# Other y buffers, an earlier copy of a half tile and later gathers in a retention and mixture-of-experts kernel

## The chip, the core and the metric

The kernel runs on one core of one Trainium2 chip. A core has TensorE (PE; its weight loads are listed apart as PEld), VectorE (DVE), ScalarE (ACT), GpSimd (POOL) and SyncE (SP, which here only issues transfers). Each engine works through its own list of instructions in order, and waits on semaphores where it needs another's result. The metric is the device time of one launch in microseconds (us), the median of several runs; lower is better.

## The reference, cut to what matters

```
x = retention(q, k, v)                      # 8 batches x 576 tokens -> x is (4608, 512)
expert_idx = argmax(normalised x @ normalised expert_emb.T / tau)   # one of 8 experts
gate_w = softmax probability of that expert
for e in range(8):
    mask = expert_idx == e
    h = relu(x[mask] @ w1[e])               # (n, 512) @ (512, 1024)
    out[mask] = gate_w[mask, None] * (h @ w2[e])   # (n, 1024) @ (1024, 512)
```

Every token goes to exactly one expert. All is float32.

## The kernel before, in words

The first part, up to about 170 us of the trace, computes the retention and the routing: each token gets a slot in its expert's table of 640 slots, five tiles of 128 (`CT` = 5). The tables `gid` and `sid` hold the token of each slot, for gathering rows of x and for scattering rows of the output. The change touches nothing there.

Then the experts 0 to 7 come one after the other, each with a first product (x by w1) and a second product (h by w2). Float32 numbers are split into a high and a low part, so that each product runs as three passes: high by high, high by low and low by high. ScalarE makes the high part by a copy, VectorE the low part by a subtraction. This is done for x (`xhigh`, `xlow`), for the weights (`w1hi`, `w1lo`, `w2hi`, `w2lo`) and for the hidden rows `hs` (`settle`).

**The first product** of experts 1 to 7 is done as 28 small products (`product(e, n, i)`: form n of 1 to 7, block i of 0 to 3) in the order of the list `ORDER`; below they are called product 1 to product 28 by their place in it. Each is six matmuls over 288, 304 or 320 columns, by the number of rows in the expert's fifth tile. For every block i, products of form 1, 6, 7 and 4 add up in one PSUM bank. After form 1, 6 and 7 ScalarE copies that bank to an SBUF buffer (`ya`, `yb` and `yc` in `follow`), VectorE adds another bank to it, and one or two products later `settle` turns it into the high and low parts of `hs`. The next product of the block writes the bank again, so it waits for the copy: product 20, which is (7, 2), waits for ScalarE's copy after product 17, which is (6, 2). The buffers are the same five `ys[0]` to `ys[4]` that hold the output tiles 0 to 4 of the second product, from which the scatters read.

**The second product** (`mm2(e, i, tasks)`) runs tile by tile. A full tile is 24 matmuls over 512 columns. ScalarE then scales the bank by the gate into `ys[i]`, and GpSimd scatters these rows to the output (`put_rows`). The fifth tile of experts 1 to 6 has a register `rest[e]`, its number of rows: over 64 it runs in full; with 1 to 64 rows it runs 16 matmuls on `ht`, a copy in which the high and the low parts of the half-filled tile stand side by side (`both_parts`, four VectorE copies at L1331); with none it is skipped. In the trace experts 1, 5 and 6 run in full, 2 and 3 run the 16 matmuls, 4 skips its tile. After the half-filled case a second scatter (`add_low`) adds the other half's rows.

**The order** is written out by hand. `mm2_plan(e)` says which tasks stand behind which third of each second-product tile: key 3 i + k stands in tile i, after 8 matmuls (k = 0), after 16 (k = 1) or after the tile's scatter (k = 2). The tasks prepare the next expert n = e + 1 (`xjoin`, `xsums`, `xhigh`, `xlow`, `w1sum`, `w1hi`, `w1lo`) and fetch the rows for the one after that (`gather`, GpSimd) and the gates (`gather_gates`). `mm1_plan` does the same between the small products, with `xturn` at product 10 for block 3 of gathered rows, at 16, 24 and 28 for the blocks 1, 2 and 4: ScalarE rearranges the gathered rows (L408) and SyncE starts their transposing transfer (L409).

Of the kernel before, what the change touches and what calls it, by code (L numbers as in the profile page):

```python
# [29 lines left out]
CT = 5  # L30
# [65 lines left out]
def retention_moe(ctx: ExitStack, tc: tile.TileContext, qk, kn, v0s, vs, w1, w2, head, cst, out):  # L96
# [28 lines left out]
    def done(ps):  # L125

        if Banks.loose is not None:
            Banks.loose.append(ps)
# [14 lines left out]
    ys = [keep.tile([P, DM], F32, name=f"y{k}") for k in range(5)]  # L143
# [216 lines left out]
    def fitted(e, i):  # L360
        return i == CT - 1 and 0 < e < NE - 1
# [189 lines left out]
    with ExitStack() as att:  # L551
# [3 lines left out]
        a1 = att.enter_context(tc.tile_pool(name="a1", bufs=1))  # L555
# [551 lines left out]
    with ExitStack() as moe:  # L1107
# [104 lines left out]
        def settle(src, f, k, queue=lows, bank=False):  # L1212

            hi, lo = (hs[:, s, f].rearrange("p (i h c) -> p h i c", h=2, c=HB)[:, k] for s in range(2))

            def low_part():
                nc.vector.scalar_tensor_tensor(  # L1217
                    out=lo, in0=part(src), scalar=0.0, in1=hi.bitcast(F32), op0=ALU.max, op1=ALU.subtract
                )
                if bank:  # L1220
                    done(src)

            def high_part():
                nc.scalar.activation(hi, part(src), AF.Relu)  # L1224
                queue.append(low_part)

            return high_part

        def settle_last():

            h, l = list(highs), list(lows)
            highs.clear()
            lows.clear()
            for task in h + l:
                task()
# [36 lines left out]
        def follow(n, i):  # L1272

            def add(out, x):
                nc.vector.tensor_tensor(out=out[:, :HC], in0=x[:, :HC], in1=out[:, :HC], op=ALU.add)  # L1275

            ya, yb, yc = ys[min(i, 1)], ys[(2, 3, 2, 4)[i]], ys[0]
            if n in (1, 6, 7):
                nc.scalar.copy({1: ya, 6: yb, 7: yc}[n][:, :HC], Y[i][:, :HC])  # L1279
            if n == 2:  # L1280
                add(ya, W[i])
                done(W.pop(i))
            elif n == 7:
                add(yc, Z[i])
            elif n == 3:
                add(yb, Z[i])
                done(Z.pop(i))
            settle_last()
            if n == 2:
                highs.append(settle(ya, i, 0))  # L1290
            elif n == 7:
                highs.append(settle(yc, NPR + i, 1, held if i == NPR - 1 else lows))
            elif n == 4:
                settle(Y.pop(i), NPR + i, 0, bank=True)()
            elif n == 3:
                highs.append(settle(yb, i, 1))
# [93 lines left out]
        def mm2_plan(e):  # L1390
            n = e + 1
            own, sums = slice(0, 1), slice(1, 3)
            if n == NE:
                return {0: [(count_beyond,)], 3: [(half_rows,)]}
            plan = {
                0: [(xjoin, n, 0)],
                1: [(xsums, n, 0), (xhigh, n, 0, own), (xlow, n, 0, own), (xjoin, n, 1), (w1sum, n, 0), (xhigh, n, 0, sums)],
                2: [(w1hi, n, 0, True), (xsums, n, 1), (xlow, n, 0, sums), (xhigh, n, 1, own), (w1lo, n, 0, True)],
                3: [(xjoin, n, 2), (xlow, n, 1, own), (xhigh, n, 1, sums)],
                4: [(w1hi, n, 0, False), (xsums, n, 2), (xlow, n, 1, sums), (w1lo, n, 0, False)],  # L1400
                5: [(xhigh, n, 2, own), (xjoin, n, 3), (xlow, n, 2, own), (xhigh, n, 2, sums)],
                6: [(w1sum, n, 1), (xhigh, n, 3, own), (xsums, n, 3), (w1hi, n, 1, True), (xjoin, n, 4)],
                7: [(w1lo, n, 1, True), (xlow, n, 3, own), (xhigh, n, 3, sums), (xsums, n, 4), (xlow, n, 2, sums)],
                8: [(xhigh, n, 4, own), (xlow, n, 4, own), (xlow, n, 3, sums), (xhigh, n, 4, sums), (w1hi, n, 1, False)],
                9: [(xlow, n, 4, sums), (w1lo, n, 1, False)],
                10: [(w1sum, n, 2)],
                11: [(w1hi, n, 2, True), (w1lo, n, 2, True)],
                12: [],
            }
            if n + 1 < NE:  # L1410
                for i in range(CT):
                    plan[(2, 4, 8, 9, 11)[i]].append((gather, n + 1, i))
            if fitted(e, CT - 1):
                plan[9].insert(1, (both_parts,))
            for k, a0, a1 in ((2, 0, 2), (5, 2, 4), (9, 4, CT)):
                plan[k].insert(0, (gather_gates, n, a0, a1))
            if n + 1 < NE:
                plan[12].append((xturn, n + 1, 0))
            if e == 0:
                plan[0] = [(xturn, 1, 4)] + plan[0]  # L1420
            return plan

        def mm1_plan(e):
            n = e + 1
            plan = {
                2: [(w2hi, e, 0)],
                3: [(w2lo, e, 0)],
                5: [(w1hi, e, 2, False)],
                6: [(w1lo, e, 2, False), (w1sum, e, 3)],
                12: [(w1hi, e, 3, True)],  # L1430
                13: [(w1lo, e, 3, True)],
                14: [(w1hi, e, 3, False)],
                15: [(w1lo, e, 3, False)],
                18: [(w2hi, e, 1)],
                19: [(w2lo, e, 1)],
                21: [(w2hi, e, 2)],
                22: [(w2lo, e, 2)],
            }
            if n < NE:
                plan[10] = [(xturn, n, 3)]  # L1440
                plan[16] = [(xturn, n, 1)]
                plan[24] = [(xturn, n, 2)]
                plan[28] = [(xturn, n, 4)]
            return plan
# [13 lines left out]
        for f, ps in zip(PAIRS, first):  # L1458
            mm1_out(f, 0, ps)

        plan = {
            4: [(w2hi, 0, 0)],
            5: [(w2lo, 0, 0)],
            6: [(xprep, 0, 3), (xprep, 0, 4), (gates_exp,)],
            7: [(w2hi, 0, 1)],
            8: [(gates_sum,), (w2lo, 0, 1)],
            9: [(w2hi, 0, 2), (gather, 1, 3), (gather, 1, 4)],
            10: [(gates_out,), (w2lo, 0, 2), (xturn, 1, 0)],
            11: [(w2hi, 0, 3)],
# [9 lines left out]
        for e in range(NE):  # L1479
            if e:  # L1480
                plan = mm1_plan(e)
                for k, (n, i) in enumerate(ORDER, 1):
                    product(e, n, i)
                    follow(n, i)
                    if k == 10 and fitted(e - 1, CT - 1):
                        add_low(e - 1)
                    if k < len(ORDER):
                        run_tasks(plan, k)
                highs.pop()()
                w2hi(e, 3)  # L1490
                lows.pop()()
                w2lo(e, 3)
                held.pop()()
                run_tasks(plan, len(ORDER))
            plan = mm2_plan(e)
            for i in range(CT):
                if (e, i) == (0, 2):
                    load_left()
                if e * CT + i == NA - 2:
                    ntile = nc.values_load(ovt[0:1, 0:1], min_val=0, max_val=NO)  # L1500
                mm2(e, i, lambda k: run_tasks(plan, 3 * i + k))
# [196 lines left out]
```

## Time and profile before

| | us |
|---|---|
| median of 3 runs (552.21 to 553.76) | 552.37 |
| the profiled execution's own time | 551.17 |
| its span, first to last instruction | 549.1 |

| engine | busy, us | share of the span |
|---|---|---|
| PE | 541.6 | 99% |
| PEld (weight loads) | 489.4 | 89% |
| DVE | 419.9 | 76% |
| ACT | 377.4 | 69% |
| POOL | 250.9 | 46% |

A row of a timeline gives start, duration, engine, line, operation, the tile written and those read, the shapes and a count of merged instructions; in brackets the engine's idle time before it and what ended that. Line numbers are those of the kernel before. The granted TensorE clock is full in all of the span. The profiled execution's time stands 2.1 us above its span and 1.2 us below the median of the runs.

### The profile page before, as it was taken

How to read it: one execution, taken by the hardware profiler on the slowest of the kernel's cores; microseconds unless marked ns; L12 is line 12 of the kernel's file. 1: busy time of each engine (PE TensorE's matmuls, PEld its weight loads, DVE VectorE, ACT ScalarE, POOL GpSimd, SP SyncE). 2: the span in 40 equal slices, each digit the busy share in tenths (PEclk: the TensorE clock that was granted, in tenths of full speed). 3: DMA queues.
4: the chain of work that ended last, by engine and by line, in shares of the span. 5: the costliest groups of instructions: out<-in, count | busy, mean ns of one | idle time of the engine just before them, and what ended most of it. 6: DMA issues, size and time to landing. Idle time of an engine off the chain costs nothing. (4 is left out here: it accounts for less than half of the span.)

```text
span 549.1 us, 13547 instructions
## 1 busy us (share of the span) xinstructions
PE 541.6 (99%) x5051; PEld 489.4 (89%) x5051; DVE 419.9 (76%) x975; ACT 377.4 (69%) x700; POOL 250.9 (46%) x239
## 2 busy tenths in 40 slices
PE   9999999999999999999999999999999999999996
PEld 8898988989898899889988987998898899889985
DVE  4856788798876957995897889689888958976810
ACT  1257454547758859977896898789789868957511
POOL 6773435553463751285057318704731851334022
PEclk9999999999999999999999999999999999999999
DMA  9999999978458474847556655675665565632111
GB/s 325 407 383 369 371 330 356 378 275 274 160 186 206 161 203 117 166 146 185 159 167 168 164 163 175 183 159 161 184 164 157 173 174 154 137 135 64 66 39 50
DMA packets 81974, 109.79 MB, mean 200 GB/s; under 512 B 43094, under 2 KB 44538, under 8 KB 81888
## 3 DMA queue, kind: packets, MB, share of 16 engines
q1 hardware_dynamic: 71920, 86.24, 51.4%
q0 software_dynamic: 8560, 20.16, 11.9%
q10 hardware_dynamic: 1408, 2.17, 1.1%
q8 instruction: 63, 1.03, 0.7%
q14 instruction: 23, 0.19, 0.1%
HBM read 80.27 MB, written 21.51 MB: 185 GB/s over the span
## 5 line engine op out<-in xcount | busy, mean ns | idle before, releaser
L1349 PE MATMUL m<-w2s,hs 128*128 128x512 f32 x552 | 127.2, 389 | 0.0
L1349 PEld LDWEIGHTS m<-w2s,hs 128*128 128x128 f32 x552 | 103.4, 188 | 21.3
L1309 POOL DMA_INDIRECT out<-y,sid x41 | 45.7, 1115 | 166.1 <-ACT y L1375 134.1
L1349 PE MATMUL a<-w2s,hs 128*128 128x512 f32 (+1 forms) x360 | 78.8, 375 | 0.0
L1349 PEld LDWEIGHTS a<-w2s,hs 128*128 128x128 f32 x360 | 64.2, 188 | 11.9
L366 POOL DMA_INDIRECT raw<-xd,gid x40 | 42.9, 1073 | 19.4 <-issue 9.3
L1224 ACT ACTIVATE hs<-y 128x320 fp32r<-128x320 f32 x84 | 39.2, 473 | 13.1 <-DVE y L1275 12.5
L415 ACT COPY raw<-raw 128x1024 uint16<-128x1024 uint16 x35 | 47.7, 1363 | 0.0
L734 POOL TENSOR_TENSOR kt<-kt,cs 128x512 f32<-128x512 f32 x28 | 28.4, 1044 | 42.1 <-DMA kt<-kn 42.1
L380 POOL DMA_INDIRECT gt<-gd,gid x34 | 39.0, 1146 | 17.2 <-issue 9.7
L1152 DVE TENSOR_TENSOR w2s<-raw,w2s 128x1024 fp32r<-128x1024 f32 x32 | 39.1, 1222 | 8.3 <-ACT w2s L1149 8.2
L1275 DVE TENSOR_TENSOR y<-a,y 128x320 f32<-128x320 f32 x53 | 25.5, 486 | 26.0 <-issue 11.4
L1217 DVE SCALAR_TENSOR_TENSOR hs<-y,hs 128x320 fp32r<-128x320 f32 x84 | 42.3, 510 | 3.3 <-ACT hs L1224 1.3
L1255 PE MATMUL m<-xsb,w0s 128*128 128x288 f32 (+2 forms) x270 | 43.8, 300 | 0.1
L1255 PE MATMUL a<-xsb,w0s 128*128 128x288 f32 (+2 forms) x270 | 43.6, 301 | 0.2 <-ACT y L1279 0.2
L1255 PEld LDWEIGHTS a<-xsb,w0s 128*128 128x128 f32 x270 | 39.2, 188 | 0.4 <-ACT y L1279 0.4
L1255 PEld LDWEIGHTS m<-xsb,w0s 128*128 128x128 f32 x270 | 39.2, 188 | 0.3 <-DVE hs L1217 0.3
L1375 ACT ACTIVATE y<-m,gt 128x512 f32<-128x512 f32 x26 | 17.8, 686 | 31.0 <-PE m L1349 31.0
L408 ACT COPY raw<-raw 128x1024 uint16<-128x1024 uint16 x35 | 36.6, 1045 | 0.0
L1149 ACT CAST w2s<-raw 128x1024 fp32r<-128x1024 f32 x32 | 33.4, 1043 | 2.4 <-DMA raw<-w 2.4
L753 POOL TENSOR_TENSOR qkt<-qkt,gsb 128x384 f32<-128x384 f32 x32 | 31.3, 1008 | 6.5 <-issue 4.2
L454 DVE TENSOR_TENSOR xsb<-raw,xsb 128x128 fp32r<-128x128 f32 x70 | 30.4, 484 | 0.0
(274 smaller groups left out, 1216.9 us busy)
## 6 DMA issues: line engine op xcount, KB each, us to landing
raw<-w SPq DMA_DIRECT2D x64, 512.0 KB
qkt<-qk SPq DMA_DIRECT2D x28, 576.0 KB
xd<-y SPq DMA_DIRECT2D x36, 256.0 KB
vt<-vs SPq DMA_DIRECT2D x7, 1152.0 KB
kt<-kn SPq DMA_DIRECT2D x7, 1024.0 KB
qkt<-qk ACTq DMA_DIRECT2D x4, 288.0 KB
qkt<-qk SPq DMA_DIRECT2D x4, 288.0 KB
out<-y,sid POOLq DMA_INDIRECT x41
```

Source lines behind the costliest of these rows:

```text
L366: nc.gpsimd.indirect_dma_start(out=t[:, XO : XO + DM], out_offset=None, in_=xd[:rows, :], in_offset=bass.IndirectOffsetOnAxis(ap=gid[:, a ...
L380: nc.gpsimd.indirect_dma_start(out=g[:, i : i + 1], out_offset=None, in_=gd[:, :], in_offset=bass.IndirectOffsetOnAxis(ap=ids, axis=0),)
L408: nc.scalar.copy(far.rearrange("p (h n) -> p h n", h=2), near.rearrange("p (n h) -> p h n", h=2))
L415: nc.scalar.copy(far.bitcast(U16).rearrange("p (n h) -> p h n", h=2), near.rearrange("p (h n) -> p h n", h=2))
L753: nc.gpsimd.tensor_tensor(out=q, in0=q, in1=gsb[:, p, :], op=ALU.mult)
L1149: nc.scalar.copy(hi, u)
L1152: nc.vector.tensor_tensor(out=lo, in0=u, in1=hi.bitcast(F32), op=ALU.subtract)
L1217: nc.vector.scalar_tensor_tensor(out=lo, in0=part(src), scalar=0.0, in1=hi.bitcast(F32), op0=ALU.max, op1=ALU.subtract)
L1224: nc.scalar.activation(hi, part(src), AF.Relu)
L1255: nc.tensor.matmul(ps[:, :n_cols], w[:, ws, ka, d * P : (d + 1) * P], xop(kx, xsp)[:, d, :n_cols], start=(n in (1, 2, 5) and d == 0 and k ...
L1309: put = nc.gpsimd.indirect_dma_start(out=out.rearrange("t (k n) -> (t k) n", k=k), out_offset=bass.IndirectOffsetOnAxis(ap=rows, axis=0), ...
L1349: nc.tensor.matmul(ps[:, :step], rows[f // NPR][:, f % NPR] if rows is ht else rows[:, f], w[:, ws, f, n : n + step], start=(m == 0), stop ...
```

## The change

Three edits in the second stage of the kernel. First, `both_parts` moves from the middle of the fourth tile to the head of the second product, behind the first eight matmuls. Second, the gathers of the blocks 2 and 3 and the last gate gather move behind the fourth tile's scatter, block 3 ahead of block 2. Third, the buffers of the first product are dealt out anew: block 1 uses `ys[1]` for both `ya` and `yb`, and blocks 2 and 3 use `ys[3]` for `ya`, which before was `yb` of block 1.

```diff
@@ -1274,7 +1274,7 @@
             def add(out, x):
                 nc.vector.tensor_tensor(out=out[:, :HC], in0=x[:, :HC], in1=out[:, :HC], op=ALU.add)
 
-            ya, yb, yc = ys[min(i, 1)], ys[(2, 3, 2, 4)[i]], ys[0]
+            ya, yb, yc = ys[(0, 1, 3, 3)[i]], ys[(2, 1, 2, 4)[i]], ys[0]
             if n in (1, 6, 7):
                 nc.scalar.copy({1: ya, 6: yb, 7: yc}[n][:, :HC], Y[i][:, :HC])
             if n == 2:
@@ -1408,11 +1408,11 @@
                 12: [],
             }
             if n + 1 < NE:
-                for i in range(CT):
-                    plan[(2, 4, 8, 9, 11)[i]].append((gather, n + 1, i))
+                for i in (0, 1, 3, 2, 4):
+                    plan[(2, 4, 11, 11, 11)[i]].append((gather, n + 1, i))
             if fitted(e, CT - 1):
-                plan[9].insert(1, (both_parts,))
-            for k, a0, a1 in ((2, 0, 2), (5, 2, 4), (9, 4, CT)):
+                plan[0].append((both_parts,))
+            for k, a0, a1 in ((2, 0, 2), (5, 2, 4), (11, 4, CT)):
                 plan[k].insert(0, (gather_gates, n, a0, a1))
             if n + 1 < NE:
                 plan[12].append((xturn, n + 1, 0))
```

VectorE at the head of a second product, where the first product's last low parts end and the next expert's sums (L426, L432) begin; `y_84` to `y_88` are `ys[0]` to `ys[4]`, `raw_77` to `raw_83` the seven buffers `raws[0]` to `raws[6]`:

```order
 L1152 TENSOR_TENSOR w2s<-raw_77,w2s 128x1024
 L1217 SCALAR_TENSOR_TENSOR hs<-y_84,hs 128x5x64
+L1331 COPY w0s<-hs 128x8x32 x4
 L426 TENSOR_TENSOR raw_78<-raw_78 128x256
 L432 TENSOR_TENSOR raw_78<-raw_78 128x128
```

The four copies into `ht` (part of `w0s`) now stand ahead of all of the next expert's sums instead of behind them.

GpSimd behind the third tile's scatter (out<-y_86), in the same second product:

```order
 L380 DMA gt<-gd,gid 128x1 x2
 L1309 DMA out<-y_86,sid 4608x512
-L366 DMA raw_80<-xd,gid 128x512
-L380 DMA gt<-gd,gidx 128x1
-L366 DMA raw_81<-xd,gid 128x512
-L1309 DMA out<-y_87,sid 4608x512
+L1309 DMA out<-y_87,sid 4608x512
+L380 DMA gt<-gd,gidx 128x1
+L366 DMA raw_81<-xd,gid 128x512
+L366 DMA raw_80<-xd,gid 128x512
 L366 DMA raw_82<-xd,gid 128x512
```

The fourth scatter (out<-y_87) moves ahead of two gathers and a gate gather, and the gathers into `raw_80` (block 2) and `raw_81` (block 3) change places.

ScalarE around products 8 to 10 of a first product; `a_` and `m_` are PSUM banks:

```order
 L1224 ACTIVATE hs<-y_85 128x5x64
 L1279 COPY y_84<-a_67 128x320
-L1279 COPY y_87<-m_70 128x320
-L1264 UNCONDITIONAL_BRANCH x5
-L1224 ACTIVATE hs<-y_84 128x5x64
-L1279 COPY y_85<-m_69 128x320
+L1264 UNCONDITIONAL_BRANCH x2
+L1279 COPY y_85<-m_70 128x320
+L1224 ACTIVATE hs<-y_84 128x5x64
+L1264 UNCONDITIONAL_BRANCH x3
+L1279 COPY y_87<-m_69 128x320
 L408 COPY raw_81<-raw_81 128x1024
```

The copies after products 9 and 10 keep their places and exchange buffers: the one after product 9 now writes `y_85`, whose low part VectorE has still to make, and the one after product 10 writes `y_87`.

## Rows read from the trace of the kernel before

**Rows 1.** Waits of PE from 165 to 545 us: total, times, longest.
```profile
PE m L1349 <- DVE w0s L1331: 0.4, 2, 0.2
PE a L1255 <- PEq L1369: 0.3, 1, 0.3
PE a L1255 <- ACT y L1279: 0.2, 1, 0.2
```
**Rows 2.** Timeline of PE, second products of experts 2 and 3.
```profile
281.70 11.04 PE L1349 MATMUL m<-w2s,hs 128*128 128x512 f32 x48
292.95 4.00 PE L1349 MATMUL m<-w2s,w0s 128*128 128x512 f32 x16 [0.21 <-DVE w0s L1331]
...
325.00 5.60 PE L1349 MATMUL a<-w2s,hs 128*128 128x512 f32 x24
330.44 11.04 PE L1349 MATMUL m<-w2s,hs 128*128 128x512 f32 x48
341.64 3.98 PE L1349 MATMUL m<-w2s,w0s 128*128 128x512 f32 x16 [0.16 <-DVE w0s L1331]
```
**Rows 3.** Timeline of DVE in the second product of expert 2.
```profile
275.75 0.43 DVE L426 TENSOR_TENSOR raw<-raw 128x256 f32<-128x256 f32 x1 [0.58 <-ACT raw L415]
...
292.21 1.05 DVE L1331 CAST w0s<-hs 128x256 fp32r<-128x256 f32 x4
```
**Rows 4.** Timeline of DVE in the first product of expert 2.
```profile
255.96 0.52 DVE L1217 SCALAR_TENSOR_TENSOR hs<-y,hs 128x320 fp32r<-128x320 f32 x1
```
**Rows 5.** Timeline of ACT in the first product of expert 2.
```profile
255.84 0.43 ACT L1279 COPY y<-a 128x320 f32<-128x320 f32 x1 [0.32 <-PE a L1255]
256.17 0.47 ACT L1224 ACTIVATE hs<-y 128x320 fp32r<-128x320 f32 x1
256.69 0.43 ACT L1279 COPY y<-m 128x320 f32<-128x320 f32 x1
...
260.03 0.47 ACT L1224 ACTIVATE hs<-y 128x320 fp32r<-128x320 f32 x1 [0.19 <-DVE y L1275]
...
262.98 0.43 ACT L1279 COPY y<-m 128x320 f32<-128x320 f32 x1
```
**Rows 6.** Timeline of ACT in the first products of experts 3, 4 and 6.
```profile
307.74 0.43 ACT L1279 COPY y<-a 128x320 f32<-128x320 f32 x1 [0.28 <-PE a L1255]
...
359.94 0.43 ACT L1279 COPY y<-m 128x320 f32<-128x320 f32 x1
...
457.46 0.42 ACT L1279 COPY y<-m 128x320 f32<-128x320 f32 x1
```
**Rows 7.** Timeline of PE at product 20 of experts 2, 4 and 6.
```profile
263.63 0.96 PE L1255 MATMUL m<-xsb,wsa 128*128 128x288 f32 x6
...
360.62 0.96 PE L1255 MATMUL m<-xsb,w0s 128*128 128x288 f32 x6
...
458.36 1.85 PE L1255 MATMUL m<-xsb,w0s 128*128 128x304 f32 x12
```
**Rows 8.** Timeline of POOL from the second product of expert 2 on.
```profile
293.44 1.77 POOL L380 DMA_INDIRECT gt<-gd,gidx  x1 [0.30 <-issue]
295.51 0.96 POOL L366 DMA_INDIRECT raw<-xd,gid  x1 [0.30 <-DVE wsum L1175]
296.77 1.01 POOL L1309 DMA_INDIRECT out<-y,sid  x1 [0.30 <-issue]
```
**Rows 9.** Timeline of ACT: fourth tile of expert 2 gated; L408 in expert 3.
```profile
292.78 0.69 ACT L1375 ACTIVATE y<-m,gt 128x512 f32<-128x512 f32 x1 [1.63 <-PE m L1349]
...
305.35 1.05 ACT L408 COPY raw<-raw 128x1024 uint16<-128x1024 uint16 x1
```
**Rows 10.** Stretch 297 to 303 us: time, busy PE, PEld, DVE, ACT, POOL, clock, DMA share, GB/s.
```profile
297.00:303.00 6.00, 6.00 (x47) 6.00 (x46) 3.16 (x5) 4.76 (x8) 3.68 (x3) 1.00 1.05 230
```
**Rows 11.** Branches of line L1264 on PE's sequencer: shortest, median, longest in ns.
```profile
L1264 PEldq COMPARE_BRANCH  x224: 70/208/1583, 193.8 to 514.3; - x112
```

## The prediction

> **What bounds the kernel now.** The table of busy times first: PE is busy in 541.6 of 549.1 us, so the time can only fall where PE waits, and can only rise where PE gets a new wait. VectorE (76%), ScalarE (69%) and GpSimd (46%) have room on average, but share their queues between work that PE waits for and work that it doesn't. The second view is the list of PE's waits in the expert stage [rows 1]: only three kinds are listed, 0.9 us together by the page's count. The two at the half-filled fifth tile end with VectorE's copies at L1331; one follows the branch at L1369 where expert 4's tile is skipped; one follows a ScalarE copy in expert 5. The third view, PE's timeline, prices them better. A tile of 24 matmuls takes 5.44 us from start to start (330.44 less 325.00), so two tiles begun at 281.70 should be over at 292.58; the 16 matmuls of expert 2 begin at 292.95, 0.37 us late. For expert 3, 330.44 and two tiles give 341.32, and it begins at 341.64, 0.32 us late [rows 2].
>
> **Edit 1, the copies at the head.** Four copies take 1.05 us; those that PE waits for at 292.95 began only at 292.21 [rows 2, 3]. At the head they stand four tiles, 21.8 us, ahead of the fifth, so this wait goes: at least the idle time that the page shows (0.21 and 0.16), at most the lateness, 0.37 + 0.32 = 0.69 us. I take 0.69, since the copies are then done long before. Nothing is behind them to take their place: the fourth tile's matmuls end at 292.58, and PE then needs only weights and `ht`. The four other fitted experts gain nothing, as PE doesn't read `ht` there. The price is VectorE's: everything from the first sums to the old place is up to 1.05 us later, less the 0.58 us for which VectorE stood idle there [rows 3], so about 0.5 us. PE needs none of that work before the next first product, and from the old place on VectorE is as early as before or earlier. I cost it at nothing; were the cover gone it would be 0.5 us for each of six experts, 3 us.
>
> **Edit 2, the gathers.** Before, the third gather, the gate gather and the gather of block 3 stood ahead of the fourth scatter, which was issued at 296.77 [rows 8], though its tile was ready at 292.78 + 0.69 = 293.47 [rows 9]. Now it goes out at about 293.8, some 3 us earlier, and its buffer `ys[3]` comes free earlier. The gather of block 3, at 295.51 before, now starts behind scatter (1.0) and gate gather (1.8) with 0.3 of issue each: 293.8 + 1.3 + 2.1 = 297.2 at most, 1.7 us later. Block 2's comes 1.3 us after that. Block 3 is wanted by ScalarE's L408 at 305.35 [rows 9], 8 us after the new issue; block 2 not before product 24. PE waits for none of the scatters. Cost nothing; the bounds are a gain of 0.3 us (the wait on ScalarE in expert 5, [rows 1]) and the late gathers below.
>
> **Edit 3, the buffers.** This is the part that adds a wait. ScalarE's copy after product 9 now writes `ys[1]`, from which VectorE still makes a low part; in expert 2 that ends at 255.96 + 0.52 = 256.48 [rows 4], and the copy ran at 255.84 [rows 5]. It has to wait some 0.65 us. Queued behind it on ScalarE are a high part and the copy after product 10. From a copy to the next instruction is 0.33 us (256.17 less 255.84), and the same again behind the high part, so the copy after product 10 starts at 256.5 + 0.66 = 257.2, against 256.69: 0.5 us later. What went before was the same wait one copy later, on the same low part, which is why the shift is 0.5 and not 0.65.
>
> How far does the 0.5 go? In expert 2 ScalarE has a single idle gap from there to the copy after product 17, 0.19 us at 260.03, and that one waits for a VectorE addition that itself follows a ScalarE copy, so it doesn't absorb it. The copy after product 17 started at 262.98 and ended at 263.41 [rows 5]; product 20, which writes the same bank, started at 263.63 [rows 7]. The slack is 0.22, the shift 0.5: a new PE wait of about 0.3. In expert 4 the copy ends at 360.37 [rows 6] and product 20 starts at 360.62 [rows 7], slack 0.25, so again about 0.25 to 0.3. In expert 3 ScalarE is idle for 0.28 us on PE before 307.74 [rows 6], which takes half of the shift, and the rest meets a like slack: nothing. In expert 6 the columns are more and PE slower: copy over at 457.88, product at 458.36 [rows 6, 7], slack 0.48, nothing; experts 1 and 5 stand like it, and expert 7 has no L408 in between. Together about 0.6 us; the bounds are 0, if the shift is absorbed, and the whole delay for all seven experts, 7 x 0.65 = 4.6 us. I take 0.6 because the rows of experts 2 and 4 show both ends of the wait.
>
> The sum: -0.69 + 0.6 = about -0.1 us. Made against the profiled execution it is 551.17 - 0.1 = 551.1; that execution stands 1.2 us below the median of the runs, so the median would go from 552.37 to 552.3.
>
> **The rivals.**
>
> *Only the gain is seen.* ScalarE's queue has small gaps that I counted as dependent; should they absorb the 0.5 us, 0.69 remain, and with expert 5's 0.3 it is 1.0 us: 551.4 to 551.7. For it speaks that PE showed only one wait on ScalarE's copies in seven first products [rows 1], against it that the slack at product 20 is 0.22 us [rows 5, 7].
>
> *ScalarE's new wait decides.* The place is the copy after product 9 in experts 1 to 7, the price up to 0.65 us each, 4.6 in all, less 0.69: 556.3. It decides from where the shift exceeds the slack at product 20 by more than PE can hide; half of the price would be 554.0. Against it speak the slack of 0.48 in expert 6 [rows 6, 7] and that nothing carries over from one expert to the next, because ScalarE catches up in PE's long tiles (1.63 us idle at 292.78, [rows 9]).
>
> *The gathers come late.* Between 297 and 303 us the transfers are at a share of 1.05, all 16 engines full [rows 10], and block 3's gather is now issued at the edge of this stretch instead of before it. If it landed only 2 us after 305.35, ScalarE would stand for that at product 10 and PE for perhaps 1 us of it, six times: 6 us, 558. Against it: even to the end of the stretch there are 2.3 us to spare. The Trainium skill, "DMA: Bandwidth & Descriptors", section "Issuing engines are not separate DMA queues", says that transfers of all issuing engines run on the same 16 engines and interleave; by that rule the later gather shares them with SyncE's transposing transfers, which makes this rival possible, and the share of 1.05 agrees with it.
>
> *The copies aren't what holds the fifth tile.* If PE meets something else at the branch, as in expert 4 where 0.3 us is put down to the sequencer [rows 1], the gain is 0 and only the 0.6 stays: 553.0.
>
> *Code loading.* ScalarE's, VectorE's and GpSimd's lists are cut anew between the branches, with a few rows more; PE's list is the same. One branch on PE's sequencer took 1.58 us where the median is 0.21 [rows 11]. Such a wait at a bad place on ScalarE in each of six experts, with half of it hidden, would be 6 x 0.8 = 4.8 us: 557. The Trainium skill, "Runtime: NRT & Kernel Launch", section "Instruction fetch mechanics", says that a taken branch whose target isn't among the loaded pages must wait for a load; by that rule each moved branch is a risk, and the 1.58 us looks like one such case, though no row shows one on ScalarE.
>
> **How the numbers follow.** A run of this kernel can tell about 0.3%, 1.66 us, from no change. My forecast of about no change has a chance of 0.50; only the gain 0.26; ScalarE's wait 0.09; late gathers 0.06; the copies not to blame 0.06; code loading 0.03. All the PE time that this change can give back is 0.69 + 0.3 = 1.0 us, less than 1.66, so faster gets only 0.06, for what the runs scatter. Slower takes most of ScalarE's wait, the late gathers and code loading and a little of the rest: 0.15. The rest, 0.79, is within 0.3%. Predicted 552.3 us; the forecast's own range is 551.6 to 553.0; the range for 8 in 10 takes in the gain alone, the scatter of the runs and the milder half of ScalarE's wait, 551.0 to 554.1.
>
> **What would show it.** Right: no wait of PE on L1331 any more, and the 16 matmuls of experts 2 and 3 start 10.88 us after the third tile; the copy after product 9 starts as the low part ends, product 20 of experts 2 and 4 waits for ScalarE by 0.2 to 0.4 us; the fourth scatter is issued 3 us earlier and ScalarE's L408 at product 10 doesn't wait. Wrong: an idle ScalarE before that L408, PE waits on ScalarE's copies in most experts, or a span that changes by more than 1.7 us.

## The result, and the profile after

The changed kernel takes 555.47 us (median of 22 runs, 553.43 to 560.93), the kernel before in the same runs 551.96 us: a ratio of 1.0073, with a 95% interval of 1.0058 to 1.0087. It is slower by 0.7%, outside the predicted range. Its profiled execution took 557.73 us, span 555.9 against 549.1.

That execution is one of the slower ones, with a span 6.8 us longer where the medians lie 3.5 us apart, so what follows accounts for one execution and not for the median. Where the 6.8 us went is read by PE's starts. "PE's loss" is below the sum, over the matmuls of the seven first products, of what two starts lie further apart than usual in that stage.

| stretch of the profiled execution | before | after | difference |
|---|---|---|---|
| start to the first product of expert 1 | 197.83 | 199.80 | +1.97 |
| PE's loss in the seven first products | 0.90 | 6.72 | +5.82 |
| late starts of the two half-filled fifth tiles | 0.69 | 0.00 | -0.69 |
| all the rest | | | -0.3 |

The first line is code that the change doesn't touch. It varied between 196.5 and 200.1 us over the fourteen kernels of this study, and what part of it is chance stays open. The other lines are the change. PE's list of waits in the expert stage, which was three short lines [rows 1], is now (total, times, longest):

```profile
PE m L1255 <- ACT y L1279: 1.9, 5, 0.5
PE a L1255 <- ACT y L1279: 0.8, 3, 0.4
PE a L1255 <- PEq L1369: 0.3, 1, 0.3
PE a L1255 <- issue: 0.2, 1, 0.2
```

The two waits on L1331 are gone; there are eight waits on ScalarE's copies (L1279) instead of one. PE's timeline at the fifth tiles of experts 2 and 3, which answers to [rows 2]:

```profile
285.50 11.05 PE L1349 MATMUL m<-w2s,hs 128*128 128x512 f32 x48
296.38 3.89 PE L1349 MATMUL m<-w2s,w0s 128*128 128x512 f32 x16
...
335.62 11.05 PE L1349 MATMUL m<-w2s,hs 128*128 128x512 f32 x48
346.50 3.90 PE L1349 MATMUL m<-w2s,w0s 128*128 128x512 f32 x16
```

Both begin 10.88 us after the third tile, to the hundredth: edit 1 gave all of its 0.69 us. The loss is in the first products. ScalarE in expert 2, where the copy after product 9 is the first row (it answers to the first three of [rows 5]) and the copy after product 17 the last:

```profile
259.84 0.43 ACT L1279 COPY y<-a 128x320 f32<-128x320 f32 x1 [1.83 <-DVE hs L1217]
260.16 0.47 ACT L1224 ACTIVATE hs<-y 128x320 fp32r<-128x320 f32 x1
260.53 0.42 ACT L1279 COPY y<-m 128x320 f32<-128x320 f32 x1
...
266.79 0.42 ACT L1279 COPY y<-m 128x320 f32<-128x320 f32 x1
```

The same place on VectorE (to [rows 4]), on POOL, and PE at product 20 (to the first of [rows 7]):

```profile
258.87 0.85 DVE L1217 SCALAR_TENSOR_TENSOR hs<-y,hs 128x320 fp32r<-128x320 f32 x1
```
```profile
258.64 1.69 POOL L1175 TENSOR_TENSOR wsum<-raw 128x256 f32<-128x256 f32 x2 [3.19 <-DVE wsa L1152]
```
```profile
267.26 1.05 PE L1255 MATMUL m<-xsb,wsa 128*128 128x288 f32 x6 [0.46 <-ACT y L1279]
```

Read them from the start of product 1, 248.44 before and 250.92 after. The low part of `ya` of block 1 ended at 8.04 before, and ends at 8.80 now. The copy after product 9 stands 0.12 behind it, at 8.92. The copy after product 10 goes from 8.25 to 9.61, the one after product 17 from 14.54 to 15.87, and product 20 from 15.19 to 16.34. So the new wait is where the prediction put it, and the chain behind it is the predicted one. But what is waited for is itself later, by 0.76 us. The copy after product 9 starts 0.1 us behind that low part in all seven experts, at 8.35 to 9.86.

Edit 2 on POOL, and the tile that the fourth scatter (first row) waited for, on ScalarE; they answer to [rows 8, 9]:

```profile
297.55 1.14 POOL L1309 DMA_INDIRECT out<-y,sid  x1 [1.84 <-ACT y L1375]
...
300.99 0.98 POOL L366 DMA_INDIRECT raw<-xd,gid  x1 [0.31 <-issue]
```
```profile
296.58 0.69 ACT L1375 ACTIVATE y<-m,gt 128x512 f32<-128x512 f32 x1 [1.50 <-PE m L1349]
...
405.19 0.42 ACT L1279 COPY y<-m 128x320 f32<-128x320 f32 x1
407.09 1.05 ACT L408 COPY raw<-raw 128x1024 uint16<-128x1024 uint16 x1 [1.49 <-DMA raw<-xd,gid]
```

The scatter goes out 0.28 us after its tile is ready, and the gather of block 3 follows 3.44 us later, both as worked out. In expert 5 the last row shows that this gather came too late: L408 at product 10 stood 1.49 us for it. In the other experts L408 follows the copy before it without a gap.

One more loss stands in expert 4: product 15 starts 0.40 us late, 0.51 with the next matmul, behind a branch of line L1267 on PE's sequencer (shortest, median and longest in ns):

```profile
361.78 1.07 PE L1255 MATMUL a<-xsb,w0s 128*128 128x288 f32 x6 [0.23 <-issue]
```
```profile
L1267 PEldq COMPARE_BRANCH  x252: 65/176/1825, 196.1 to 521.8; - x126
```

### The profile page after: what moved, and what is told of

Same layout as the page of the kernel before. It is cut to its first block, busy times and chain, and to the rows that moved or that the text cites. A ratio compares the mean times of both kernels' runs of the same rounds, so it can differ in the third digit from the quotient of the medians.

```text
span 555.9 us, 13555 instructions
## 1 busy us (share of the span) xinstructions
PE 544.2 (98%) x5051; PEld 489.5 (88%) x5051; DVE 419.8 (76%) x975; ACT 375.3 (68%) x700; POOL 252.2 (45%) x239
## 4 chain that ended last, share of the span: by engine, by line
PE 68%; DMA 9%; ACT 8%; DVE 6%; issue 5%; POOL 2%; POOLq 0%; SPq 0%; ACTq 0%
PE m L1349 18%; PE a L1349 11%; PE a L1255 7%; DMA out<-y,sidx 6%; PE m L1255 5%; PE a L763 4%; PE m L763 2%; PE a L846 2%; ACT hs L1224 2%; PE m L465 2%; PE a L465 2%; PE m L846 2%; ACT w0s L1149 2%; DVE y L1275 2%; PE a L929 1%
## 5 line engine op out<-in xcount | busy, mean ns | idle before, releaser
L366 POOL DMA_INDIRECT raw<-xd,gid x40 | 44.3, 1108 | 19.4 <-issue 9.4
L380 POOL DMA_INDIRECT gt<-gd,gid x34 | 40.2, 1183 | 17.1 <-issue 9.8
L408 ACT COPY raw<-raw 128x1024 uint16<-128x1024 uint16 x35 | 36.6, 1047 | 1.5 <-DMA raw<-xd,gid 1.5
```

What stands on the lines that cost most here:

```text
L366: nc.gpsimd.indirect_dma_start(out=t[:, XO : XO + DM], out_offset=None, in_=xd[:rows, :], in_offset=bass.IndirectOffsetOnAxis(ap=gid[:, a ...
L380: nc.gpsimd.indirect_dma_start(out=g[:, i : i + 1], out_offset=None, in_=gd[:, :], in_offset=bass.IndirectOffsetOnAxis(ap=ids, axis=0),)
L408: nc.scalar.copy(far.rearrange("p (h n) -> p h n", h=2), near.rearrange("p (n h) -> p h n", h=2))
```

## The experiments

For the first four runs, theory A: the y buffers alone make the loss. B: the later gathers do. C: it takes both. Then H: PE's completion signals come late where gathers run at the start of a stage. W: the new wait costs the same whatever the transfers do. V: the moved copies make VectorE late. The last column of the table is the stretch from the first product of expert 1 to that of expert 7, which leaves out the first part and the end.

| kernel | ratio to before, 95% interval | PE's loss, us | stretch, us |
|---|---|---|---|
| before | 1 | 0.90 | 295.30 |
| changed | 1.0073, 1.0058 to 1.0087 | 6.72 | 300.14 |
| y_only | 1.0039, 1.0018 to 1.0060 | 3.80 | 298.16 |
| no_y | 1.0002, 0.9977 to 1.0028 | 3.75 | 297.18 |
| copies_only | 1.0080, 1.0053 to 1.0106 | 5.88 | 299.29 |
| gathers_only | 1.0029, 1.0005 to 1.0052 | 0.87 | 294.96 |
| after_no_late | 1.0070, 1.0044 to 1.0097 | 1.93 | 295.37 |
| copies_no_late | 1.0054, 1.0037 to 1.0072 | 0.10 | 293.58 |
| spread | 1.0036, 1.0013 to 1.0058 | 3.86 | 299.28 |
| after_spread | 1.0031, 1.0016 to 1.0045 | 3.04 | 296.71 |
| before_extra | 1.0054, 1.0035 to 1.0072 | 2.63 | 296.52 |
| late4 | 1.0043, 1.0028 to 1.0059 | 3.73 | 297.27 |
| spread_no_y | 1.0044, 1.0028 to 1.0061 | 2.63 | 298.14 |
| spread8 | 1.0179, 1.0134 to 1.0225 | 11.63 | 305.10 |

The losses and stretches are of one profiled execution each. That of gathers_only was the fastest of its 12 runs (550.38, median 554.57), that of before_extra as fast as any of its 8 (551.85, median 553.79), so these two traces show less than the medians. Those of the changed kernel (557.73, median 555.47), spread (556.22, median 553.08) and spread_no_y (554.86, median 553.10) were slow ones and show more.

**One edit alone, and all but one.** y_only:

```diff
-            ya, yb, yc = ys[min(i, 1)], ys[(2, 3, 2, 4)[i]], ys[0]
+            ya, yb, yc = ys[(0, 1, 3, 3)[i]], ys[(2, 1, 2, 4)[i]], ys[0]
```

> The kernel before with the y buffers alone. Theory A (the buffers do it): ScalarE's copy after product 9 waits for VectorE's low part in all seven experts, product 20 waits for ScalarE in most of them, PE loses 3 to 6 us in the first products, no wait on L1331 goes; 555 to 558 us, ratio 1.006 to 1.010. Theory B (the later gathers do it, by making the work around product 5 late): the low part of ya(1) ends 8.0 to 8.3 us after product 1 as before, the loss stays at the 0.6 us of the forecast; ratio 1.000 to 1.002. Theory C (it takes both: the buffers add the wait, the gathers make what is waited for late): about half, ratio 1.002 to 1.005.

no_y is the changed kernel with this line as it was.

> The changed kernel with the y buffers of before: copies at the head and late gathers remain. Theory A: the 0.7 us of the two fifth tiles is gained and nothing is lost, 551 to 552 us, ratio 0.998 to 1.000, PE's loss in the first products near the 0.9 us of before. Theory B: the loss stays, ratio 1.005 to 1.008. Theory C: the work around product 5 is late, but without the new wait it costs little; ratio 0.999 to 1.002, copies after product 5 late in experts 1, 2, 3 and 6 as in the changed kernel.

copies_only:

```diff
-                plan[9].insert(1, (both_parts,))
+                plan[0].append((both_parts,))
```

> The kernel before with VectorE's copies at the head alone. All theories: no wait of PE on L1331, 16 matmuls of experts 2 and 3 start 10.88 us after the third tile, -0.7 us, ratio 0.9980 to 1.0000. Should the moved copies make VectorE's low parts late in the next first products (a rival of its own), PE's loss there would be above 2 us and the ratio 1.001 or more.

gathers_only:

```diff
-                for i in range(CT):
-                    plan[(2, 4, 8, 9, 11)[i]].append((gather, n + 1, i))
+                for i in (0, 1, 3, 2, 4):
+                    plan[(2, 4, 11, 11, 11)[i]].append((gather, n + 1, i))
...
-            for k, a0, a1 in ((2, 0, 2), (5, 2, 4), (9, 4, CT)):
+            for k, a0, a1 in ((2, 0, 2), (5, 2, 4), (11, 4, CT)):
```

> The kernel before with the order of the gathers and the fourth scatter alone. Theory A: nothing, ratio 0.999 to 1.001, waits on L1331 as before. Theory B: 3 to 6 us slower, ratio 1.005 to 1.010, ScalarE waits at L408 behind product 10 or at the copy after product 5. Theory C: the copy after product 5 and the low part of ya(1) are late by 0.5 us in several experts, and PE loses 1 us or less; ratio 1.000 to 1.002.

None of the three theories holds as it stood. C comes nearest: the buffers alone cost 0.39%, less than A asks for and more than B and the forecast, and taking them out of the changed kernel (no_y) brings it back to the time of before, with PE's loss at 3.75 us and not at the 0.9 of A. The gathers alone cost 0.29%; in that trace the copy after product 5 is 0.6 to 0.7 us late in experts 1, 2 and 6, as C has it. But the copies alone, which I had costed at nothing, cost 0.80%, the most of the three, as only the rival V allowed, and with the gathers beside them (no_y) that is gone. The edits don't add up.

PE's first rows in expert 3 of copies_only, then ScalarE's and VectorE's:

```profile
298.20 1.76 PE L1255 MATMUL a<-xsa,w0s 128*128 128x288 f32 x12
...
304.80 1.07 PE L1255 MATMUL a<-xsb,w0s 128*128 128x288 f32 x6 [0.81 <-ACT y L1279]
```
```profile
298.40 0.69 ACT L1375 ACTIVATE y<-m,gt 128x512 f32<-128x512 f32 x1 [1.37 <-PE m L1349]
300.87 0.43 ACT L1279 COPY y<-a 128x320 f32<-128x320 f32 x1 [1.78 <-PE m L1255]
```
```profile
296.96 0.95 DVE L1152 TENSOR_TENSOR w0s<-raw,w0s 128x768 fp32r<-128x768 f32 x1
303.11 0.49 DVE L1275 TENSOR_TENSOR y<-a,y 128x320 f32<-128x320 f32 x1 [5.21 <-ACT w2s L1149]
```

The first row is products 1 and 2, six matmuls each over some 0.8 us, so product 1 is through at about 299.2 and product 2 at 300.0. ScalarE is free from 299.09, and needs nothing but product 1 for the copy; it starts at 300.87. VectorE is free from 297.9, and needs that copy (over at 301.30) and product 2 for its addition; it starts at 303.11. Both waited for PE's signal that a product is done, and it came 1.7 and 3.1 us behind the product's end. The trace's record of PE's semaphore agrees: product 1's update stands at 300.84, and those of products 2 to 6 follow together between 303.03 and 303.34. VectorE's own order, which edit 1 changes, was long through. With that, V looked weak and H was formed: what is late is not work, but signals, where late gathers, the scatters, a weight load and the transposing transfer fall together. In expert 7, which has neither gathers nor a transposing transfer behind it, no signal was late in any kernel.

Late signals aren't new with the change. ScalarE's copies after products 4 and 5 in expert 5 of the kernel before:

```profile
394.65 0.43 ACT L1279 COPY y<-m 128x320 f32<-128x320 f32 x1
396.19 0.43 ACT L1279 COPY y<-a 128x320 f32<-128x320 f32 x1 [1.11 <-PE m L1255]
```

From product 1 at 390.05 they stand at 4.60 and 6.14, against 4.18 and 4.77 in copies_no_late (below), and the low part of `ya` of block 1 ends 1.17 us later than there. The one wait on ScalarE's copies in [rows 1], product 8 of that expert, goes with it.

**Without the late transfers.** after_no_late and copies_no_late leave out three gathers of each expert from 2 on, as their expectations say:

```diff
         t = xg[e, i] = raws[(2, 3, 6)[i]] if (e, rows) == (0, BEG) else raws[(i + 1) % 7]
+        if e > 1 and i > 1:
+            return
```

> The changed kernel without the gathers of blocks 2, 3 and 4 of experts 2 to 7 (their rows stay what the buffers held). Theory H: PE's completion signals are held up where these transfers run in the first five microseconds of a stage of first products, so that VectorE's low part ends late, and edit 3's new wait on ScalarE then passes the delay on. Then the copy after product 5 stands 4.2 to 4.4 us after product 1 in all seven experts, the low part of ya(1) ends at 8.0 to 8.3, the copy after product 9 still starts 0.1 us behind it, and PE's loss in the first products falls from 6.7 to 1.5 to 2.5 us (0.5 in each of experts 2, 3 and 4); 551.5 to 553 us, ratio 0.998 to 1.001. Theory W: the new wait alone makes the loss, whatever the transfers do; PE's loss stays at 5 to 7 us, ratio 1.005 to 1.008.

> The kernel before with the copies at the head, without the gathers of blocks 2, 3 and 4 of experts 2 to 7. Theory H: the 1.8 to 1.95 us that PE lost in each of experts 3, 4 and 5 go, PE's loss in the first products is 0.6 us or less, the fifth tiles' 0.7 us stay gained; 550.5 to 552 us, ratio 0.996 to 0.999. Theory V (the moved copies make VectorE late, not the transfers): the copy after product 5 and the low parts stay 1 to 2.5 us late in experts 3 to 5, ratio 1.006 to 1.010.

The two added lines move the line numbers by two. The first steps of expert 3 in copies_no_late, on ScalarE and VectorE, and the whole list of PE's waits from 165 to 545 us:

```profile
298.71 0.43 ACT L1281 COPY y<-a 128x320 f32<-128x320 f32 x1
```
```profile
299.57 0.49 DVE L1277 TENSOR_TENSOR y<-a,y 128x320 f32<-128x320 f32 x1 [2.15 <-ACT y L1281]
```
```profile
PE a L1257 <- PEq L1371: 0.3, 1, 0.3
```

Product 1 starts at 297.72, so these stand at 0.99 and 1.85 us, against 2.67 and 4.91 with the gathers in. PE loses 0.10 us in seven first products: V falls, and H holds in that no signal is late without the gathers. Leaving them out takes away GpSimd's issuing as well as the transfers, so which of the two holds up the signals isn't shown. In after_no_late the copy after product 5 stands at 4.23 to 4.77 in all seven experts, the low part ends at 8.04 to 8.29 (8.78 in expert 5), and what is left is edit 3, with the new places of the gate gather and the fourth scatter. Its PE waits, then ScalarE's copies after products 9 and 10 and PE's product 20, all of expert 2:

```profile
PE m L1257 <- ACT y L1281: 0.7, 3, 0.3
PE a L1257 <- PEq L1371: 0.3, 1, 0.3
```
```profile
258.88 0.43 ACT L1281 COPY y<-a 128x320 f32<-128x320 f32 x1 [1.07 <-DVE hs L1219]
259.20 0.47 ACT L1226 ACTIVATE hs<-y 128x320 fp32r<-128x320 f32 x1
259.57 0.42 ACT L1281 COPY y<-m 128x320 f32<-128x320 f32 x1
```
```profile
266.30 1.06 PE L1257 MATMUL m<-xsb,wsa 128*128 128x288 f32 x6 [0.23 <-ACT y L1281]
```

From product 1 at 250.72: the copy after product 10 at 8.85, 0.60 later than before (predicted 0.5), product 20 at 15.58, 0.39 late; its second matmul adds 0.10, and one in product 28 another 0.07. PE loses 0.56, 0.58 and 0.60 us in experts 2, 3 and 4, and 0.10 or less in each of the others.

The times of these two kernels missed: 1.0070 and 1.0054 where 1.001 and 0.999 were the most. Their stretches are as expected, but the end, from expert 7's first product on, took 59.8 us in both profiles against 56.0 in the kernels before and after: the last scatter landed 2.3 us after its issue in all of them, but the DRAIN that closes GpSimd's list took 7.0 us instead of 3.4, for a reason left open. These 3.8 us are 0.7%, more than all that copies_no_late is slower. The first part took 1.4 to 2.2 us more than in before.

**The late gathers somewhere else.** spread keeps every gather, and moves two of them into the next first product. Against copies_only:

```diff
-                for i in range(CT):
-                    plan[(2, 4, 8, 9, 11)[i]].append((gather, n + 1, i))
+                for i in (0, 1, 3):
+                    plan[(2, 4, 8, 8)[i]].append((gather, n + 1, i))
...
                 plan[24] = [(xturn, n, 2)]
+                if e > 0:
+                    plan[11] = [(gather, n, 2)]
+                    plan[17] = [(gather, n, 4)]
```

> The kernel before with the copies at the head, and with the gathers of blocks 2 and 4 issued behind products 11 and 17 instead of at the end of the second product. Theory H: two transfers fewer in the first five microseconds; the signals are late in fewer experts, PE loses 1 us or less in the first products and gains 0.7 in the fifth tiles; 550.5 to 552 us, ratio 0.996 to 1.000. Theory V: as the copies alone, ratio 1.006 to 1.010. If the new places of the gathers are too late for product 24 (L408), ScalarE waits there and the ratio is above 1.003.

after_spread is the changed kernel with the gathers of blocks 2 and 4 at the same new places.

> The changed kernel with the gathers of blocks 2 and 4 behind products 11 and 17. Theory H: as the changed kernel without its late gathers, with that of block 3 left: the copy after product 9 waits for the low part in all seven experts, PE's loss 1.5 to 3.5 us, ratio 0.999 to 1.004, and 0.002 to 0.005 above the same placing with the y buffers of before. Theory W: ratio 1.005 to 1.008.

As H has it, in both the copy after product 5 is on time in all seven experts, and the changed kernel falls from 1.0073 to 1.0031. Of its loss, 1.76 us are in experts 2, 3 and 4, mostly at product 20, but for 0.42 in expert 4 at product 15 behind a branch of 1.97 us; 1.20 are in expert 5, behind the late gather of block 3. But spread isn't faster than before. Its loss is one place, product 28 of expert 4; PE, and the branches of line L1267 on PE's sequencer (shortest, median and longest in ns):

```profile
370.84 1.81 PE L1255 MATMUL a<-xsb,wsa 128*128 128x288 f32 x6 [2.90 <-issue]
```
```profile
L1267 PEldq COMPARE_BRANCH  x252: 65/176/3865, 195.0 to 520.0; - x126
```

One branch took 3.87 us instead of 0.18, and PE ran dry behind it. Whether it does so in every run isn't known.

**More traffic in the kernel before.** before_extra:

```diff
+        spare = tc.dram_tile([NE * P, DM], F32, name="spare")
+        def store_more(e):
+            nc.sync.dma_start(
+                out=spare[e * P : (e + 1) * P, :].rearrange("p (k n) -> p k n", n=P),
+                in_=ident.unsqueeze(1).broadcast_to([P, DM // P, P]),
+            )
...
+                plan[11].append((store_more, n + 1))
```

> The kernel before with one edit: 256 KB more are written from a constant tile to memory that nothing reads, behind the weight load that SyncE issues as a stage of first products begins (six times). Theory H (transfers that fall together at the stage's start make PE's signals late): ScalarE's and VectorE's steps behind products 1 to 5 are 0.5 to 3 us late in some experts that were on time, PE loses 2 to 6 us in the first products, ratio 1.003 to 1.010. Theory W (only the new wait costs): nothing but noise, PE's loss near 0.9, ratio 0.999 to 1.001.

The time is as H has it, 1.0054 with no edit of the change in the kernel. The place isn't: in its trace no step behind products 1 to 5 is later than in before by more than 0.05 us. The losses are 0.7 at product 15 of expert 2 and 0.5 at product 12 of expert 3, both behind long branches on PE's sequencer (2.66 and 1.73 us), and 1.3 at product 24 of expert 5, where ScalarE's copy after product 21 stood 2.30 us for a scatter (`add_low`). So the store made no signal late in this trace, and that late signals come from any transfer is not shown; they went with the gathers.

late4 is copies_only with block 4's gather alone behind product 8:

> The kernel before with the copies at the head and with block 4's gather alone moved, to behind product 8 of the next first products. Theory H: one of the three late transfers less at the stage's start; steps behind products 1 to 5 on time in at least four of the six experts, PE's loss in the first products 1.5 us or less against 5.9 with the copies alone, 0.7 gained in the fifth tiles; ratio 0.997 to 1.001. Theory V (the moved copies make VectorE late): as the copies alone, 1.006 to 1.010.

Five of the six experts that had gathers behind them are on time up to product 5 or nearly so (one addition 0.7 late in expert 3); in expert 5 the copies after products 4 and 5 are 0.8 and 1.7 us late. The loss of 3.73 and the ratio of 1.0043 are more than expected: 0.8 each in experts 3 and 4 at products 12 and 15, both behind a branch of 2.0 us, and 2.1 in expert 5.

**A version that beats both?** spread_no_y is after_spread with the buffers line of before.

> The changed kernel with the gathers of blocks 2 and 4 behind products 11 and 17 and the y buffers of before: only edit 3 is taken from the kernel that had those places. Theory H: no step behind products 1 to 5 is late, the copy after product 9 stands at 7.4 to 7.7 us as before, the 0.56 to 0.60 us at product 20 of experts 2, 3 and 4 go; PE's loss in the first products 1.5 us or less, all of it in expert 5; 0.002 to 0.004 below the same kernel with edit 3, ratio 0.998 to 1.001. If edit 3 costs nothing once the transfers are out of the way, the two kernels are equal, ratio 1.002 to 1.004. Should it beat the kernel before, it is the best version here.

The trace shows what H expected up to product 27: the copy after product 9 at 7.37 to 8.23, no loss in experts 2 and 3. Then product 28 of expert 4 comes 2.43 us late behind a branch of 3.25 us, as in spread. By time it can't be told from after_spread, so there edit 3's price is seen in the trace alone.

spread8 puts both gathers of spread behind product 8:

```diff
-                    plan[11] = [(gather, n, 2)]
-                    plan[17] = [(gather, n, 4)]
+                    plan[8] = [(gather, n, 2), (gather, n, 4)]
```

> The kernel before with the copies at the head, and the gathers of blocks 2 and 4 both behind product 8 of the next first products: the same as the first spreading, some 3 us earlier, so that the transfers are over before product 28. Theory H: nothing late behind products 1 to 5; and if the branch of 3.9 us at product 28 of expert 4 came from the gathers' place, it goes: PE's loss in the first products under 1.5 us, 0.7 gained in the fifth tiles, ratio 0.996 to 1.000, the best version here. If PE's code is late at that branch whatever the gathers do, 2 to 4 us are lost there again and the ratio is 1.002 to 1.005.

The long branch is gone there, and it is the slowest kernel of all. POOL and then ScalarE in expert 2:

```profile
257.70 0.99 POOL L366 DMA_INDIRECT raw<-xd,gid  x1 [0.15 <-issue]
259.00 1.41 POOL L366 DMA_INDIRECT raw<-xd,gid  x1 [0.30 <-DVE y L1275]
260.71 2.68 POOL L1309 DMA_INDIRECT out<-y,sidx  x1 [0.30 <-issue]
```
```profile
267.77 0.42 ACT L1279 COPY y<-m 128x320 f32<-128x320 f32 x1 [3.30 <-DMA out<-y,sidx]
```

Both gathers now stand ahead of the scatter of the half-filled tile's low rows (`add_low`, the third row), which reads `ys[4]`; ScalarE's copy after product 21 writes `ys[4]`, and waits for it until 267.77. PE loses 2.6 to 4.1 us in each of experts 2, 3 and 4. I had not named what is queued behind the moved gathers. No version here beats the kernel before.

## Why the prediction was wrong, step by step

- *Edit 1's gain, 0.69 us.* Right, to the hundredth.
- *"I cost it at nothing"* (edit 1's price on VectorE). The reasoning on VectorE was right, the step was wrong: the copies alone cost 0.80%, though with the late gathers beside them (no_y) the time was that of before. In experts 3 and 4 SyncE's weight load and transposing transfer go out 0.3 us earlier as counted from product 1 (the load 0.26 before it, where it was 0.08 behind it), and PE's signals come 1 to 3 us late there and in expert 5. That the gathers are needed for it is shown by copies_no_late, where the losses go; that this shift is the trigger is only argued.
- *Edit 2, "cost nothing".* The issue times were right to 0.1 us. The gather of block 3 was late for L408 in expert 5, 1.49 us on ScalarE, where the prediction had looked at expert 3's row alone: expert 4's fifth tile is skipped, so expert 5's stage begins a tile sooner behind the same transfers (argued from the order, not tried). after_spread still loses 1.20 us there, after_no_late 0.10.
- *Edit 3, "about 0.6 us".* This is the step that failed, and the term that was mis-sized most. The mechanism was right: copy after product 9 on the low part, the shift to product 20. The size was taken from one execution in which the low part was on time in experts 2, 3 and 4, and from two experts alone. Undisturbed, its price is 1.8 us (after_no_late 1.93, copies_no_late 0.10): the shift is 0.60 instead of 0.5, later matmuls add 0.17, and expert 3 was taken to absorb it on a gap of 0.28 us, which was no slack of its own: before, product 12 of expert 3 came 0.26 us late behind the long branch of [rows 11]. Without that, its copy after product 17 stands at 14.50 (copies_no_late), like that of expert 2. Experts 1, 5, 6 and 7 cost nothing, as predicted.
- *The low part's end was taken as fixed.* In the changed kernel it is 0.2 to 1.7 us later in experts 1 to 4 and 6, since signals behind products 2 to 7 are late and the low part, then beside POOL's sums in four of these experts, lasts 0.85 us and not 0.5. In expert 5, where it had been late before, it ends 1.17 us earlier. The wait in expert 5 of [rows 1] was the sign that it can be late, and the prediction read it only as something to gain. With the buffers of before ScalarE meets it one copy later, and PE loses less of it. In the traces edits 1 and 2 give 2.85 us (no_y against before), edit 3 on top of them 2.97 (changed against no_y): together the 5.82.
- *The rivals.* "ScalarE's new wait decides" (556.3, or 554.0 at half price) named the place, and 555.5 lies between; it got 0.09. What I held against it, the slack of 0.48 at product 20 of expert 6, was read from a stage in which nothing was late; in the changed kernel that product came 0.43 us late. "The gathers come late" was right in expert 5 alone. "Code loading" was priced on ScalarE; on PE, long branches cost the changed kernel 0.51 us (expert 4) and the kernel before 0.37 (expert 3), so it explains little of the change, but it made most of the loss in spread and spread_no_y.

What stays open: by which path the gathers hold up PE's signals, whether by GpSimd's issuing or by the transfers, and why that costs time in experts 3, 4 and 5 of copies_only and in expert 5 alone of before, whose issue times differ by 0.3 us in experts 3 and 4. The 1.97 us of the first part are not explained either. Leaving out the transposing transfers was not tried.

## What to carry to other kernels

A slack that one trace shows is the slack of that run: before adding a wait to a queue that PE follows, ask how late the thing waited for can get, not only when it was done last time. Transfers that gather at a stage's start deserve a look of their own: here an edit that gained 0.69 us elsewhere was slower by 0.80% with them, and without the gathers PE lost 0.10 us in the first products. A single odd wait in the old trace is worth following to its source before the same engine gets a new one. Moving a transfer past others means naming, for each one behind it in the queue, the buffer that it frees and who writes that next.

## What the runs showed of the hardware

- PE's completion signals can come up to 3 us late while PE itself runs at its usual pace: in copies_only ScalarE and VectorE stood free for 1.7 and 1.8 us with all they needed done, and not in copies_no_late. In before it shows in expert 5 (1.1 us at the copy after product 5). The list of waits shows nothing of it at the place (PE doesn't wait there), only its result three or more products later.
- VectorE's low part took 0.85 or 0.86 us beside POOL's sums (in expert 2 two additions of 1.69 together) in experts 1, 2, 3 and 6 of the changed kernel, and 0.48 to 0.49 where no addition of POOL ran. The Trainium skill, "SBUF — State Buffer", section "Who interferes with whom", says that a VectorE instruction with two inputs in SBUF contends with a GpSimd instruction that reads SBUF. The low part reads two such inputs, and the trace agrees.
- A branch of PE took 3.87 us in spread and 3.25 in spread_no_y, where the median is 0.18. The packets of the instruction queue show 16 KB of code that began to move 0.8 us after each of these two branches began. The branch of 1.83 us in the changed kernel has such a packet too, begun 0.65 us before it. The Trainium skill, "Runtime: NRT & Kernel Launch", section "Instruction fetch mechanics", says that a taken branch whose target isn't loaded waits for a fetch of it; the cases of spread and spread_no_y agree.
